# Moving one pair's ordering and DMA transposes from the first part to the end of step 10

## The chip, the cores and the metric

The kernel runs on one core of one Trainium2 chip. The metric is the device time of one execution in microseconds (us). A profiled execution also has a span, which in these runs is 1.8 us shorter than the time (411.0 against 412.8 us in the profile of before). TensorE is called PE, VectorE DVE, ScalarE ACT, GpSimd POOL, SyncE SP. PSUM is the memory, in banks, that PE writes its results into.

## The reference

Attention for 8 batches of 12 heads (sequence 448, head size 64), with one extra `exp(-m)` in the softmax denominator, then two matrix layers with an exact GELU between them:

```python
scores = scale * np.matmul(q, k.transpose(0, 1, 3, 2))
m = np.max(scores, axis=-1, keepdims=True)
e = np.exp(scores - m)
attn = e / (np.sum(e, axis=-1, keepdims=True) + np.exp(-m) + 1e-09)
attn_out = np.matmul(attn, v)
x = attn_out.transpose(0, 2, 1, 3).reshape(B * S, H * D)     # 3584 x 768
h = x @ w_in                                                 # 768 x 2048
out = (0.5 * h * (1.0 + erf(h / sqrt(2)))) @ w_out           # 2048 x 768
```

## The kernel before

The work goes in steps, one per pair of heads (6 pairs per batch, 48 steps). A step's scores run on PE between pieces of the matrix layers of the batch before. From batch 2 on, q and k are transposed by DMA rather than by PE. For batch 2 they first have to be put in order by pairs on DVE, into borrowed memory: buffers `hbuf0` and `hbuf1`, which hold the first layer's output in other phases, and a small tile `order`.

```python
PARTS = (0, 3, 4, NPAIR)          # batch 2: pairs 0-2, pair 3, pairs 4-5

def fetch_part(b, i):
    c0, c1 = PARTS[i:i + 2]
    for w in range(2):            # q, then k
        order_by_pairs(b, w, c0, c1, (1, 0, None)[i])   # hbuf1, hbuf0, order
        transpose_on_dma(b, w, c0, c1)                  # issued by SyncE
...
# fetch_part(2, 0) before step 8; parts 1 and 2 inside steps 12 and 13
```

The second layer's tiles of batch 0 go through a pool of output buffers (`osb_pool`). The stores of the second layer's first three tiles of batch 0 (steps 8 to 10) are held, and go out on SyncE together with step 11's own:

```python
if b == 0 and nh == 0:
    held.append(store)
else:
    store()
    for f in held:
        f()
    held.clear()
```

So after step 11 all four buffers wait for eight stores, and step 12's copy into a fifth tile needs one of them back.

The softmax here doesn't subtract the row's maximum and nothing guards it: scores larger than these inputs give would overflow.

Of the kernel before, what the change touches and what calls it, by code (L numbers as in the profile page):

```python
# [10 lines left out]
FP16 = mybir.dt.float16  # L11
# [8 lines left out]
def kernel(  # L20
# [11 lines left out]
    B, H, S, D = q.shape  # L32
    DM = H * D
    DFF = moe_w_in.shape[1]
    P = 128
    NJ = 4
    PS = S // NJ
    NK = S // P
    NPAIR = H // 2
# [6 lines left out]
    NBURST = 8  # L46
# [19 lines left out]
    h_pool = ctx.enter_context(tc.tile_pool(name="h_pool", bufs=1))  # L66
# [37 lines left out]
    def load_pairs(tiles, name, src, b):  # L104

        n, nj = (PS, NJ) if src is q else (P, NK)
        tiles[b] = raw_pool.tile([n, H, nj, D], FP16, name=name)
        if b == 3:
            nc.vector.memset(tiles[b][:, 0, 0, 0:1], 0.0)
        dst = tiles[b].rearrange("p h j d -> p (h j d)").rearrange(  # L110
            "p (c j e d) -> p c j e d", c=NPAIR, j=nj, e=2)
        view = src[b, :, 0:n * nj].rearrange("(c e) (p j) d -> j e p c d", e=2, j=nj)
        for j in range(nj):
            for e in range(2):
                nc.gpsimd.dma_start(out=dst[:, :, j, e, :], in_=view[j, e])  # L115
# [9 lines left out]
    def load_left(tiles, src, b):  # L125

        n = 2 if b else 1
        view = src[b, :, NFULL:S].rearrange("(c i e) s d -> i e s c d", i=n, e=2)
        for i in range(n):
            dst = tiles[b % 2].rearrange("p (c i) x -> p i c x", i=n)[:, i]  # L130
            for e in range(2):
                x = slice(e * D, (e + 1) * D) if src is k else slice(0, D)
                nc.gpsimd.dma_start(out=dst[left_rows(b, i, e), :, x], in_=view[i, e])  # L133
# [25 lines left out]
    def load_q(b, *heads):  # L159
        load_heads(q_raw, raw_pool, "rawq", q, b, *heads)  # L160

    def load_k(b, *heads):
        load_heads(k_raw, raw_pool, "rawk", k, b, *heads)

    def load_v(b, *heads):
        load_heads(v_t, v_pool, "vn", v, b, *heads)
# [96 lines left out]
    def transpose_on_pe(b, c, main=True, left=True):  # L263
        tp = ps_bank.tile([P, S + NFULL + P], FP16, name="bank")
        if main:
            for e in range(2):
                r = slice(e * D, (e + 1) * D)
                for j in range(NJ):
                    nc.tensor.transpose(
                        tp[r, j * PS:(j + 1) * PS], q_raw[b][:, 2 * c + e, j, :], ident[0:PS, 0:PS])  # L270
            for e in range(2):
                r = slice(e * D, (e + 1) * D)
                for j in range(NK):
                    nc.tensor.transpose(
                        tp[r, S + j * P:S + (j + 1) * P], k_raw[b][:, 2 * c + e, j, :], ident)
        if left:
            for e in range(2):
                r = slice(e * D, (e + 1) * D)
                nc.tensor.transpose(tp[r, S + NFULL:], kl_raw[b % 2][:, c, r], ident)
        x = slice(0 if main else S + NFULL, S + NFULL + P if left else S + NFULL)  # L280
        nc.vector.tensor_copy(
            out=qt_t[b].rearrange("p (c x) -> p c x", c=NPAIR)[:, c, x], in_=tp[:, x])

    ordered = [{}, {}]

    def order_by_pairs(b, w, c0, c1, buf):

        nj, raw = ((NJ, q_raw), (NK, k_raw))[w]
        if w == 0:
            n = 2 * (c1 - c0)  # L290
            if buf is not None:
                spare = h_pool.tile([P, NBURST * S], FP16, name=f"hbuf{buf}")
            else:
                spare = order_pool.tile([P, n * (NJ + NK) * D], FP16, name="order")
            for i, (rows, chunks, x) in enumerate(((PS, NJ, 0), (P, NK, n * NJ * D))):
                ordered[i][b] = spare[0:rows, x:x + n * chunks * D].rearrange(
                    "p (h j d) -> p h j d", h=n, j=chunks)
        src = raw[b].rearrange("p (c e) j d -> p c e j d", e=2)
        dst = ordered[w][b].rearrange("p h j d -> p (h j d)").rearrange(
            "p (c j e d) -> p c j e d", j=nj, e=2, d=D)  # L300
        for e in range(2):
            nc.vector.tensor_copy(out=dst[:, :, :, e, :], in_=src[:, c0:c1, e])

    def transpose_on_dma(b, w, c0=0, c1=NPAIR):
        if b not in qt_t:
            alloc_qt(b)
        nj, raw = ((NJ, q_raw), (NK, k_raw))[w]
        raw = ordered[w].get(b, raw[b])
        nc.sync.dma_start_transpose(
            out=dma_views(b)[w][:, c0:c1].rearrange("p c (j s) -> p (c j) s", j=nj),  # L310
            in_=raw.rearrange("p h j d -> p (h j d)"),
        )
        if w == 1 and c0 == 0:
            nc.sync.dma_start_transpose(
                out=dma_views(b)[2], in_=kl_raw[b % 2].rearrange("p c x -> p (c x)"))
# [333 lines left out]
    def mlp1(b, f0, f1):  # L649
        return [lambda mid=None, fc=fc: layer1(b, fc, mid=mid) for fc in range(f0, f1)]  # L650

    def take(n):
        got = l2[:n]
        del l2[:n]
        return got

    def gelu_window(b, n):

        load_table(SET_GELU)
        ready = take(len(l2))  # L660
        for f in ready:
            f()
        if not ready:
            for i in range(FCH - n):
                if i < n:
                    gelu_burst(b, i, i + 1)
                layer1(b, n + i, direct=True)
        else:
            for f0 in range(0, n, n // 2):
                gelu_burst(b, f0, f0 + n // 2)  # L670
            for fc in range(n, FCH):
                layer1(b, fc, direct=True)
        load_table(SET_LN_EXP)
        l2.extend(layer2_items(b))
# [5 lines left out]
        start_step(s)  # L680
    PARTS = (0, 3, 4, NPAIR)

    def load_part(i):
        load_q(2, 2 * PARTS[i], 2 * PARTS[i + 1])
        load_k(2, 2 * PARTS[i], 2 * PARTS[i + 1])
# [17 lines left out]
    stage_left(v, 1, gate=True)  # L703
    stage_left(k, 2, gate=True)
    load_part(0)
    for i in range(2):
        load_w_out(0, i, 2)
# [3 lines left out]
    cast_left(v, 1)  # L711
    cast_left(k, 2)
    load_part(1)
    load_v(1, 8, H)
    load_part(2)
    first, second = mlp1(0, 0, 2)
    first()
# [4 lines left out]
    add_up(4)  # L722

    def fetch_part(b, i):
        c0, c1 = PARTS[i:i + 2]
        for w in range(2):
            order_by_pairs(b, w, c0, c1, (1, 0, None)[i])
            transpose_on_dma(b, w, c0, c1)

    def fetch(b, r):  # L730

        if r == (0 if b else 2) and b + 2 < B:
            load_v(b + 2)
            load_left(vl, v, b + 2)
        if b == 0 and r == -1:
            fetch_part(2, 0)
        elif b and r in (0, 1) and b + 2 < B:
            transpose_on_dma(b + 2, r)
        if r == 3 and b + 3 < B:
            load_pairs(q_raw, "rawq", q, b + 3)  # L740
            load_pairs(k_raw, "rawk", k, b + 3)
            load_left(kl_raw, k, b + 3)

    step(NPAIR + 1, mlp1(0, 2, 6))
    gelu_window(0, 6)
    fetch(0, -1)
    for s in range(NPAIR + 2, NSTEP + 1):
        b, r = divmod(s - 2 - NPAIR, NPAIR)

        half = NBURST // 2  # L750
        if b and r < 2:
            step(s, mlp1(b, half * r, half * (r + 1)))
        else:
            left = len(l2) - (0 if b == 0 else 1 if b % 2 == 0 else 2)
            n = left if r == NPAIR - 1 else max(1, left // (NPAIR - r))
            if b and r == 2:
                n = 2
            step(s, take(n), late=(s == NSTEP or r == (2 if b else 0)),
                 then=(lambda: fetch_part(2, r - 3)) if b == 0 and r in (4, 5) else None)
        if b == 0 and r == 0:  # L760
            transpose_on_pe(1, NPAIR - 1)
        fetch(b, r)
        if b and r == 1:
            gelu_window(b, 2 * half)
# [41 lines left out]
```

## Time and profile before

| | before |
|---|---|
| time, median of the 3 runs given first (lowest to highest) | 411.38 us (410.46 to 411.83) |
| the profiled run: time, span | 412.8 us, 411.0 us |
| PE busy | 396.9 us, 97% |
| PE idle between 54 and 90 us | 2.3 us, 1.79 of it in one hole at 71.5 to 73.3 us |

PE is back to back after 90 us, so the table is read from its idle time before that. The lines themselves stand in the prediction.

### The profile page before, as it was taken

To read this page: it belongs to the slowest core of one execution; us is meant where nothing else is said; L and a number is where in the kernel's file an instruction comes from. 1 tells how busy PE (TensorE), PEld (TensorE's weight loads), DVE (VectorE), ACT (ScalarE), POOL (GpSimd) and SP (SyncE) were. 2 spreads that over 40 slices of the span, in tenths; PEclk is the share of its full clock that TensorE was granted. 3 is DMA by queue.
4 is the path that set the end of the run, shared out by engine and by line. 5 is a ranking of instruction groups with operands and counts; after the bars stand their busy time and mean duration, and the time that the engine had idled before them with its cause. 6 is when DMAs were issued, how large, how long until landed. Compare 5 with 4: busy or idle time off the path is not lost.

```text
span 411.0 us, 11090 instructions
## 1 busy us (share of the span) xinstructions
PE 396.9 (97%) x4711; PEld 245.8 (60%) x4711; DVE 199.5 (49%) x486; ACT 297.8 (72%) x451; POOL 120.3 (29%) x168
## 2 busy tenths in 40 slices
PE   6889999899999999999999999999999999999996
PEld 2445865556656665666666666566566565565664
DVE  3887336683366614674256813576046732530021
ACT  5999889779797747978687756988588766634300
POOL 8752313477552381056400563030000000000000
PEclk9999999999999999999999999999999999999999
DMA  9999999999994995289921999149012010110022
GB/s 162 159 189 203 193 189 161 192 156 172 147 165 86 147 181 53 60 124 136 128 59 59 161 134 101 53 99 151 21 40 60 22 41 2 59 50 11 2 80 77
DMA packets 137634, 44.02 MB, mean 107 GB/s; under 512 B 118704, under 2 KB 137584, under 8 KB 137584
## 3 DMA queue, kind: packets, MB, share of 16 engines
q0 software_dynamic: 90352, 22.19, 60.6%
q1 hardware_dynamic: 46288, 20.44, 28.1%
q10 hardware_dynamic: 944, 0.67, 0.7%
q8 instruction: 37, 0.61, 0.6%
q14 instruction: 13, 0.11, 0.1%
HBM read 45.61 MB, written 11.01 MB: 138 GB/s over the span
## 4 chain that ended last, share of the span: by engine, by line
PE 79%; DMA 15%; POOL 3%; issue 1%; DVE 0%; ACT 0%; POOLq 0%; DVEq 0%
PE bank L261 63%; DMA w_out_sb<-in_moe_w_out_dram 7%; PE st L362 6%; PE bank L411 5%; DMA w_in_sb<-in_moe_w_in_dram 5%; DMA rawq<-in_q_dram 2%; PE st L433 2%; PE st L261 2%; DMA tqk<-hbuf 2%; PE bank L426 1%; POOL rawk L99 1%; PE st L411 1%; POOL rawq L99 1%; POOL w_in_sb L173 0%; POOL klraw L133 0%
## 5 line engine op out<-in xcount | busy, mean ns | idle before, releaser
L261 PE MATMUL bank<-xt,w_in_sb 128*64 128x448 f16 x1536 | 152.1, 353 | 0.5 <-DVE xt L449 0.5
L350 ACT ACTIVATE et<-st,expb 128x896 f16<-128x896 f32 x144 | 134.4, 1005 | 24.2 <-PE st L362 23.8
L261 PEld LDWEIGHTS <-w_in_sb 128*64 128x64 f16 x1536 | 93.7, 110 | 54.3 <-issue 3.7
L261 PE MATMUL bank<-w_out_sb,gt_odd 128*64 128x384 f16 (+1 forms) x1056 | 88.1, 321 | 0.0
L530 DVE COPY osb<-bank 128x384 f32<-128x384 f32 (+1 forms) x56 | 31.0, 554 | 102.4 <-PE bank L261 102.0
L261 PEld LDWEIGHTS <-gt_odd 128*64 128x64 f16 x1056 | 58.8, 110 | 26.8 <-issue 2.1
L261 PE MATMUL bank<-w_out_sb,gt_even 128*64 128x384 f16 x768 | 68.8, 327 | 1.8 <-DMA w_out_sb<-in_moe_w_out_dram 1.8
L449 DVE TENSOR_TENSOR xt<-bank,rec 128x448 f16<-128x448 f32 x43 | 26.9, 625 | 75.1 <-PE bank L426 64.5
L261 PEld LDWEIGHTS <-gt_even 128*64 128x64 f16 x768 | 43.1, 110 | 24.4 <-issue 5.3
L473 ACT ACTIVATE gt_odd<-bank 128x448 f16<-128x448 f32 (+1 forms) x74 | 29.2, 394 | 21.7 <-PE bank L261 20.8
L362 PE MATMUL st<-tqk 64*64 64x448 f16 x576 | 41.8, 363 | 1.3 <-ACT et L350 0.4
L440 ACT ACTIVATE rec<-st,oneb 128x448 f32<-128x448 f32 x43 | 27.4, 639 | 16.8 <-PE st L433 16.0
L478 DVE COPY hbuf<-bank 128x448 f32<-128x448 f32 x54 | 33.5, 621 | 10.3 <-PE bank L261 8.7
L396 DVE TENSOR_TENSOR ksum<-ksum,el 64x448 f16<-64x448 f16 x96 | 37.0, 385 | 2.1
L115 POOL DMA_DIRECT2D rawq<-in_q_dram x40 | 30.6, 773 | 24.6 <-DMA vn<-in_v_dram 24.2
L99 POOL DMA_DIRECT2D vn<-in_v_dram x11 | 10.4, 947 | 88.2 <-PE bank L411 77.8
L396 DVE TENSOR_TENSOR ksum<-t,et 128x448 f16<-128x448 f16 x96 | 33.5, 384 | 0.7 <-ACT et L350 0.4
L396 DVE TENSOR_TENSOR t<-et 128x448 f16<-128x448 f16 x96 | 32.9, 385 | 1.0 <-ACT et L350 0.6
L473 ACT ACTIVATE gt_even<-bank 128x384 f16<-128x384 f32 x34 | 16.7, 491 | 22.1 <-PE bank L261 22.1
L411 PE MATMUL bank<-et,vn 128*64 128x448 f16 x258 | 32.2, 356 | 0.0
L350 ACT ACTIVATE el<-st,expb 128x448 f16<-128x448 f32 x48 | 30.8, 641 | 0.1
L362 PEld LDWEIGHTS <-tqk 64*64 64x64 f16 x576 | 15.3, 106 | 21.7 <-issue 17.4
(66 smaller groups left out, 284.7 us busy)
## 6 DMA issues: line engine op xcount, KB each, us to landing
vn<-in_v_dram POOLq DMA_DIRECT2D x6, 576.0 KB, 9.7
rawq<-in_q_dram POOLq DMA_DIRECT2D x40, 84.0 KB, 8.1
rawk<-in_k_dram POOLq DMA_DIRECT2D x33, 96.0 KB, 6.8
w_in_sb<-in_moe_w_in_dram POOLq DMA_DIRECT2D x4, 768.0 KB, 15.9
out_dram<-osb SPq DMA_DIRECT2D x15, 168.0 KB, 2.2
out_dram<-osb SPq DMA_DIRECT2D x16, 144.0 KB, 2.1
out_dram<-osb SPq DMA_DIRECT2D x16, 120.0 KB, 2.0
w_out_sb<-in_moe_w_out_dram POOLq DMA_DIRECT2D x2, 768.0 KB, 28.0
```

What stands on the lines that cost most here:

```text
L99: nc.gpsimd.dma_start(out=tiles[b][:, h0:h1], in_=src[b, h0:h1, 0:n * nj].rearrange("h (p j) d -> p h j d", j=nj),)
L115: nc.gpsimd.dma_start(out=dst[:, :, j, e, :], in_=view[j, e])
L261: nc.tensor.matmul(out[x], lhs[:, x], rhs, start=start, stop=stop)
L350: nc.scalar.activation(out=out, in_=in_, func=AF.Exp, bias=expb, scale=scale)
L362: nc.tensor.matmul(st[cols, e, 0:S], kt[r, j, cols], qt[r], start=True, stop=True)
L396: nc.vector.tensor_tensor(out=dst, in0=a, in1=x, op=ALU.add)
L411: nc.tensor.matmul(po_t[g][e * D:(e + 1) * D, 0:S], v_t[b][:, 2 * c + e, j, :], et[:, 2 * j + e], start=(first and j == 0), stop=(not firs ...
L440: nc.scalar.activation(out=rec_t[g], in_=den_t.pop(g)[:, 0:S], func=AF.Ln, bias=oneb, scale=1.0)
L449: nc.vector.tensor_tensor(out=xt_t[b][:, c, :], in0=po_t.pop(g)[:, 0:S], in1=rec_t.pop(g), op=ALU.mult)
L473: nc.scalar.activation(out=dst[:, 0, :], in_=ph[:, c0:c1], func=AF.Gelu)
L478: nc.vector.tensor_copy(out=h_t[b, i][:, n, :], in_=ph[:, 0:S])
L530: nc.vector.tensor_copy(out=osb[:, x:x + w], in_=po[:, 0:w])
```

## The change

Its intent: fewer DMA transposes beside the loading of w_out, by taking batch 2's third pair (pair 2) out of the first part. It is put in order and transposed at the end of step 10, when w_out has nearly landed. It shares hbuf0 with pair 3.

```diff
-    def order_by_pairs(b, w, c0, c1, buf):
+    def order_by_pairs(b, w, c0, c1, buf, x0):
...
+            x0 *= 2 * (NJ + NK) * D          # place inside the borrowed buffer
...
+    ORDERS = ((0, 2, 1, 0), (2, 3, 0, 0), (3, 4, 0, 1), (4, NPAIR, None, 0))
...
     def fetch_part(b, i):
-        c0, c1 = PARTS[i:i + 2]
+        c0, c1, home, x = ORDERS[i]
...
         if b == 0 and r == -1:
             fetch_part(2, 0)
+        elif b == 0 and r == 2:              # end of step 10
+            fetch_part(2, 1)
...
-                 then=(lambda: fetch_part(2, r - 3)) if b == 0 and r in (4, 5) else None)
+                 then=(lambda: fetch_part(2, r - 2)) if b == 0 and r in (4, 5) else None)
```

More of the change, by code (lines that the diff above doesn't have):

```diff
@@ L284 @@
     ordered = [{}, {}]
-    def order_by_pairs(b, w, c0, c1, buf):
+    spares = {}
+    def order_by_pairs(b, w, c0, c1, buf, x0):
         nj, raw = ((NJ, q_raw), (NK, k_raw))[w]
@@ L290, in order_by_pairs @@
             n = 2 * (c1 - c0)
-            if buf is not None:
-                spare = h_pool.tile([P, NBURST * S], FP16, name=f"hbuf{buf}")
+            if x0:
+                spare = spares[buf]
+            elif buf is not None:
+                spare = spares[buf] = h_pool.tile([P, NBURST * S], FP16, name=f"hbuf{buf}")
             else:
                 spare = order_pool.tile([P, n * (NJ + NK) * D], FP16, name="order")
-            for i, (rows, chunks, x) in enumerate(((PS, NJ, 0), (P, NK, n * NJ * D))):
+            x0 *= 2 * (NJ + NK) * D
+            for i, (rows, chunks, x) in enumerate(((PS, NJ, x0), (P, NK, x0 + n * NJ * D))):
                 ordered[i][b] = spare[0:rows, x:x + n * chunks * D].rearrange(
@@ L724, in fetch_part @@
     def fetch_part(b, i):
-        c0, c1 = PARTS[i:i + 2]
+        c0, c1, home, x = ORDERS[i]
         for w in range(2):
-            order_by_pairs(b, w, c0, c1, (1, 0, None)[i])
+            order_by_pairs(b, w, c0, c1, home, x)
             transpose_on_dma(b, w, c0, c1)
```

## The prediction

> **What bounds the kernel now.** I read the engine totals first. TensorE (PE) is busy 97% of the 411.0 us span, so only its 14.1 idle us can be won by moving transfers. I then cut the span into stretches and asked for each engine's busy time in each.
>
> ```profile
> PE 396.9 (97%) x4711; PEld 245.8 (60%) x4711; DVE 199.5 (49%) x486; ACT 297.8 (72%) x451; POOL 120.3 (29%) x168
> 0.00:54.00 54.00, 46.14 (x546) 28.29 (x548) 34.27 (x88) 46.05 (x80) 29.19 (x45) 0.97 1.29 182
> 54.00:70.00 16.00, 15.55 (x205) 9.27 (x202) 8.13 (x21) 15.15 (x23) 3.23 (x4) 1.00 1.37 175
> 70.00:74.00 4.00, 2.21 (x30) 1.50 (x26) 1.21 (x4) 3.07 (x5) 1.07 (x2) 1.00 2.06 119
> 74.00:86.00 12.00, 12.00 (x152) 6.99 (x149) 9.39 (x30) 10.76 (x15) 5.37 (x9) 1.00 1.58 189
> ```
>
> Columns of the last four: stretch, length, busy PE, weight loads, DVE, ACT, POOL, granted clock, DMA share, GB/s. Of PE's idle time 7.9 us lie before 54 us, where the change touches nothing. The change acts from 50 to 90 us, and there PE has one hole: 70 to 74, with 4.00 - 2.21 = 1.79 us idle. The chain of waits, in order of time, says what ends it and what comes next.
>
> ```profile
> 46.44 26.83 DMA w_out_sb<-in_moe_w_out_dram
> 73.27 0.04 issue
> 73.31 0.84 PE bank L261 x8
> ...
> 81.05 6.22 DMA tqk<-hbuf
> 87.28 0.04 DVEq L478
> 87.31 0.04 issue
> 87.36 0.64 DVE hbuf L478
> 87.99 0.04 issue
> 88.03 1.11 PE bank L261 x9
> ```
>
> So there are two transfer deadlines. At 73.3 PE waits for the last piece of w_out (step 11's half of the second layer needs it). At 87.3 VectorE (DVE) may not overwrite hbuf0 before the transpose of pair 3 has read it; DVE waited 0.73 us there. The third matmul group of step 14 needs the PSUM bank which that copy empties. PE loses almost nothing today, but the place has no slack: the copy ends at 88.00, the group starts at 88.03. After 90 us PE is back to back, so what is won or lost before 90 stays in the total.
>
> Then the DMA queues, microsecond by microsecond (three answers: 53 to 54, 66 to 67, 75 to 76; packets, MB, share).
>
> ```profile
> q0 software_dynamic: 425, 0.20, 150.4%
> ...
> q0 software_dynamic: 215, 0.13, 88.5%
> q1 hardware_dynamic: 217, 0.06, 41.1%
> ...
> q0 software_dynamic: 490, 0.19, 159.6%
> ```
>
> q0 carries the loads, w_out among them; q1 carries SyncE's transposes and stores. When q1 has transposes they go packet for packet with q0 (215 against 217), and q0 falls from 425 to 490 packets a us to about 200 to 250. First q1 packets: in the 55 to 56 slice, though the transpose was issued at 51.34; they run to about 72.7, just before w_out lands.
>
> **What the Trainium skill says.** "DMA: Bandwidth & Descriptors", section "Queues, rings and completion order", says that each DMA engine takes the queues in turn, packet by packet. The trace agrees: 215 beside 217. Its section "Issuing engines are not separate DMA queues" says that all queues share the same 16 engines; the halved q0 agrees. Its section "Latency and other measured facts" gives the hardware queue about 0.6 us to the first byte; here a store issued at 74.78 moves its first packet after 78, some 4 us later, with q0 full. The same section gives a DMA transpose 261 GB/s; here it moves 0.05 to 0.06 MB per us, some 55 GB/s, beside q0. I use the trace's values.
>
> **The change part by part.** No work is added but two small transposes' issue and two more DVE copies: at 50 us the four ordering copies become shorter, and four new ones stand on DVE's list after step 10's sums.
>
> (a) Removed at 50 to 55 us: pair 2's share of the copies, one third of 2 x 550 + 2 x 444 ns = 0.66 us. PE does not wait for DVE there: worth 0.
>
> (b) Removed from q1 before 73 us: pair 2 is 448 x 128 x 2 bytes of q and 384 x 128 x 2 of k, 213 KB, or 832 packets of 256 B. q1's first part is now 1344 + 1152 + 768 = 3264 packets (q, k, and the leftover rows of k), and becomes 2432. Summing q1's packets by us, number 2432 passes at 68.0. From there q0 would run alone. It still moves about 1146 packets, 0.5 MB, from 68.0 to the landing at 73.3; at the 0.2 MB per us that it has alone, that is 2.6 us. w_out would land near 70.7 instead of 73.3. PE needs it at about 71.5 (eight matmuls of the half start at 70.70 and last 0.82 us). So the 1.79 us should all or nearly all go.
>
> (c) Added on DVE at about 70.5: pair 2's four copies, as long as pair 3's today (two of q 0.35 us together, two of k 0.41 us: 0.7 us with the overlap). They precede step 10's last sums, which PE needs only in step 12, 6 us later; DVE is idle from 71.2 to 74.2. Worth 0.
>
> (d) Added on SyncE: two transposes issued at 70.9 and 72.1 (1.2 to 1.3 us each, as pair 3's). With a 4 us lag their first packets move near 75, after w_out. At some 250 packets a us beside q0 they take 3.3 us, to 78.2, and land near 79. PE first needs pair 2 in step 14, at 83.6: no wait.
>
> (e) The same two transposes now stand in front of the eight held stores. These are issued on eight completion semaphores in turn, each wait being for the transfer eight places back. In the new order the seventh and eighth stores wait for pair 2's q and k to land. Today the eight go out from 74.78 to 78.5, and pair 3's transpose waits for the first of them to land, 4.9 us after issue, so goes at 79.76. In the new kernel PE is 1.8 us earlier, so the first store goes at 73.4; its data queue behind pair 2 until 78.2, it lands at 78.3 to 79.4; the eighth store goes at 78.4 to 79.3. Pair 3's q transpose goes then at 78.9 to 79.7 rather than 79.76, its k 1.3 us later, and lands 6.2 us after that, at 86.4 to 87.2 rather than 87.3.
>
> (f) Sum. The first deadline frees 1.8 us of PE; the second comes only 0.1 to 0.9 us earlier and has no slack. PE then idles in step 14 for what is left, about 1.3 us. The gain is the smaller of the two: about 0.5 us. From the 411.38 median that makes 410.8.
>
> **The rivals.** First: the gain is kept whole, 1.8 us, 409.6. For it: if loads finish 2 us sooner, the stretch 77 to 84 is less crowded, and stores and pair 3 can land faster than today's 4.9 and 6.2 us. Against: the 4 us lag of q1 shows at each start in the loaded stretch, and total DMA work is the same. Second: the wait at 87.3 gets longer, as pair 2's packets are put before the stores and pair 3: with another us of delay 412.3. For it: q1 stands idle from about 68 or 70 to 75, and what it misses it must do later. Against: the stores are issued 1.4 us earlier. Third: the w_out wait does not shrink, as q0's packets are small at its end and a near standstill (87 q0 packets from 73 to 74) is not explained by q1; then the time stays at 411.4. Against: the standstill begins as w_out lands, so it does not delay it. A fourth, DVE too late for PE's banks in step 11, would cost at most the 0.7 us of the new copies; DVE's idle time after 71.2 speaks against it.
>
> **Range and chances.** Nothing here can move the time by 2% (8.2 us): PE holds 396.9 us of it, and both waits are under 2 us. Both deadlines in full, with the runs' own spread (410.46 to 411.83), give 409.5 to 412.1. Within 2%: 0.99.
>
> **What would show it right or wrong.** PE's hole in 70 to 74 falls from 1.79 us to under 0.4, and w_out lands before 72. q1's first part ends near 68. SyncE shows transposes at 70 to 73.5. The DVE copy into hbuf0 waits longer for the transpose than 0.73 us, 1.5 to 2.5, and PE shows a hole of about 1.3 us between 84 and 88. If that copy starts before 86.0, the first rival holds; if the chain still has w_out landing after 73, step (b) is wrong; if the copy starts after 88, the second rival holds.

## The result, and the profile after

The changed kernel took 412.66 us in the median (412.42 to 413.58, 4 runs), against 411.4 us for before (4 runs). The ratio is 1.0038, 95% interval 1.0014 to 1.0061. A ratio here is the mean time of one kernel's runs over that of the other's of the same rounds, so it is not quite the ratio of the medians quoted. In this call the change cost about 0.4%, and the prediction's range (409.5 to 412.1) did not hold the result.

The profile seems to say the contrary: its span is 410.6 us, shorter than before's 411.0. First the page's engine line, then the stretches that the prediction used (stretch, length, busy PE, weight loads, DVE, ACT, POOL, granted clock, DMA share, GB/s), of the changed kernel:

```profile
PE 396.8 (97%) x4711; PEld 245.9 (60%) x4711; DVE 199.3 (49%) x490; ACT 297.6 (72%) x451; POOL 120.1 (29%) x168
0.00:54.00 54.00, 46.38 (x548) 28.59 (x549) 33.44 (x88) 46.14 (x80) 29.00 (x45) 0.97 1.32 187
54.00:70.00 16.00, 15.55 (x206) 9.32 (x204) 8.38 (x22) 15.26 (x21) 3.86 (x5) 1.00 1.41 176
70.00:74.00 4.00, 4.00 (x54) 2.36 (x52) 2.79 (x11) 3.96 (x7) 2.54 (x4) 1.00 1.60 193
74.00:86.00 12.00, 10.26 (x126) 5.86 (x124) 8.36 (x26) 10.36 (x14) 6.59 (x10) 1.00 1.94 159
```

The hole of 1.79 us at 70 to 74 is gone, and one of 1.74 us has come between 74 and 86. The changed kernel's chain of waits tells where it comes from (start, length, what; lines of code from 286 on are numbered 5 higher than in before):

```profile
73.11 0.64 DVE xt L454
73.75 0.39 SPq L499
74.14 0.06 issue
74.19 5.47 DMA out_dram<-osb
79.78 0.56 DVE osb L535
...
82.61 0.39 DVE ksum L401
83.03 0.57 DVE osb L535
83.65 0.38 PE bank L431 x2
```

Step 12's copy of its output tile (L535, at 79.78) waits for a store that was issued at 74.19, because that store still reads the output buffer which the copy takes over. What comes next on DVE starts only after that copy (step 13's at 83.03), and at 83.65 PE gets the PSUM bank that step 13's copy has emptied. DVE and PE lines of the changed kernel's timeline, with the idle time before the instruction and what ended it in brackets:

```profile
79.78 0.56 DVE L535 COPY osb<-bank 128x384 f32<-128x384 f32 x1 [2.35 <-DMA out_dram<-osb]
83.65 0.38 PE L431 MATMUL bank<-el,vl 64*64 64x448 f16 x2 [1.74 <-DVE osb L535]
```

The same copy in the timeline of before:

```profile
79.98 0.56 DVE L530 COPY osb<-bank 128x384 f32<-128x384 f32 x1 [0.32 <-PE st L362]
```

It started at nearly the same time there. The profile puts its short wait down to PE, but the second store (issued at 75.19, 4.7 us to landing) landed at 79.90: the output buffers had no slack in before either. In the changed kernel step 11's output copy was 2.2 us earlier, and the landing of the second store (79.66) only 0.2 us.

Why the store was not earlier shows in SyncE's issues, of before and then of the changed kernel:

```profile
74.78 3.74 SPq L494 DMA_DIRECT2D out_dram<-osb  x8
79.76 1.19 SPq L309 DMA_TRANSPOSE tqk<-hbuf  x1
```

```profile
70.58 2.93 SPq L314 DMA_TRANSPOSE tqk<-hbuf  x2
73.60 5.82 SPq L499 DMA_DIRECT2D out_dram<-osb  x8
79.55 1.18 SPq L314 DMA_TRANSPOSE tqk<-hbuf  x1
```

SyncE is busy issuing pair 2's two transposes until 73.51. In before the first store left 0.59 us after step 11's output copy began (74.19 to 74.78), here 1.62 us (71.98 to 73.60). It then took 5.9 us to land instead of 4.9, landing after pair 2's transposes (78.62 and 79.03), which stand before it in the queue q1; run b3 below tests this order. One store even waited 1.2 us for pair 2 to land.

The DMA queues confirm the aim of the change. Of the changed kernel, from 66 to 67 and from 70 to 71 us:

```profile
q0 software_dynamic: 260, 0.11, 86.2%
q1 hardware_dynamic: 257, 0.07, 49.4%
...
q0 software_dynamic: 483, 0.19, 154.7%
```

The last packet of q1's first part is at 68.7, and from there q0 runs alone until pair 2's first packets at 73.8. The last piece of w_out landed at 70.56.

### The profile page after: what moved, and what is told of

Same layout as the page of the kernel before. It is cut to its first block, busy times and chain, and to the rows that moved or that the text cites. A ratio compares the mean times of both kernels' runs of the same rounds, so it can differ in the third digit from the quotient of the medians. Undisturbed runs are those within 1.5% of the kernel's fastest.

```text
span 410.6 us, 11100 instructions
## 1 busy us (share of the span) xinstructions
PE 396.8 (97%) x4711; PEld 245.9 (60%) x4711; DVE 199.3 (49%) x490; ACT 297.6 (72%) x451; POOL 120.1 (29%) x168
## 4 chain that ended last, share of the span: by engine, by line
PE 87%; ACT 6%; DMA 3%; DVE 2%; POOL 1%; issue 1%; SPq 0%; DVEq 0%; POOLq 0%
PE bank L261 69%; PE st L367 7%; PE bank L416 6%; ACT et L355 3%; PE st L438 2%; PE st L261 2%; DMA out_dram<-osb 2%; DMA klraw<-in_k_dram 1%; PE bank L431 1%; PE st L416 1%; ACT rec L448 1%; ACT rec L445 1%; ACT el L355 1%; DVE ksum L401 1%; DVE osb L535 0%
## 5 line engine op out<-in xcount | busy, mean ns | idle before, releaser
L535 DVE COPY osb<-bank 128x384 f32<-128x384 f32 (+1 forms) x56 | 31.0, 553 | 102.7 <-PE bank L261 100.3
L261 PEld LDWEIGHTS <-gt_odd 128*64 128x64 f16 x1056 | 58.8, 110 | 26.8 <-issue 2.1
L261 PE MATMUL bank<-w_out_sb,gt_even 128*64 128x384 f16 x768 | 68.7, 327 | 0.0
L454 DVE TENSOR_TENSOR xt<-bank,rec 128x448 f16<-128x448 f32 x43 | 26.9, 625 | 74.9 <-PE bank L431 64.1
L115 POOL DMA_DIRECT2D rawq<-in_q_dram x40 | 30.6, 772 | 27.2 <-DMA vn<-in_v_dram 25.9
L448 ACT ACTIVATE rec<-rec 128x448 f32<-128x448 f32 x48 | 28.0, 586 | 0.2
```

The source lines that it names most:

```text
L115: nc.gpsimd.dma_start(out=dst[:, :, j, e, :], in_=view[j, e])
L261: nc.tensor.matmul(out[x], lhs[:, x], rhs, start=start, stop=stop)
L448: nc.scalar.activation(out=rec_t[g], in_=rec_t[g], func=AF.Exp, scale=-1.0)
L454: nc.vector.tensor_tensor(out=xt_t[b][:, c, :], in0=po_t.pop(g)[:, 0:S], in1=rec_t.pop(g), op=ALU.mult)
L535: nc.vector.tensor_copy(out=osb[:, x:x + w], in_=po[:, 0:w])
```

## The experiments

All kernels were timed in 5 rounds beside before. Calls ran on different chips: a and b on one, c and d on another, e on a third. Only a, c and e had a full set of fresh runs of before (11); b and d had one each, and their ratios use those of a and c besides.

**a1: before, unchanged, against itself.** No edit.

> The kernel before, unchanged, against itself. Both theories: ratio 1.000, interval within 0.3%. The profile of before had a 1.79 us hole for w_out; if the hole depends on how early the loads of the first 45 us happen to run, this profile shows another size of it (0 to 1.8 us). If the ratio is off by 0.3% or more, the 0.38% recorded for the change is within the comparison's own error.

Measured: 412.03 us (410.41 to 415.01), ratio 1.0006 (0.9968 to 1.0043). The w_out hole at 74 us was 3.16 us in this profile. So it does change from run to run.

**a2: the changed kernel again.** No edit.

> The changed kernel, unchanged, against before on the same chip. Theory A (the w_out wait of 1.8 us is traded for a wait of DVE for the first two stores, whose 4 buffers are all in use; PE loses 1.74 us in step 13): ratio 0.998 to 1.001, profile again with a hole of 1 to 2 us at 80 to 84 us. Rival (the change really costs 0.38%): ratio 1.003 to 1.005, and the profile is over 1 us longer than that of before in this same call.

Measured: 412.82 us (411.56 to 415.75), ratio 1.0027 (0.9989 to 1.0064). The DVE copy waited 1.88 us for the store, PE 1.26 us at 84.2; there was also a w_out wait of 1.2 us, in step 8. The interval alone decides nothing; the hole is there again.

**a3 and a4: five output buffers, in the changed kernel and in before.**

```diff
-    osb_pool = ctx.enter_context(tc.tile_pool(name="osb_pool", bufs=4))
+    osb_pool = ctx.enter_context(tc.tile_pool(name="osb_pool", bufs=5))
```

> The changed kernel with 5 output buffers instead of 4, so that step 12's copy waits for no store. Theory A: the 2.3 us wait of DVE at 79.8 and PE's 1.7 us hole go, until the next deadline (hbuf0 read by pair 3's transpose, or step 13's copy which now waits for the same two stores); 0.5 to 1.7 us faster than the changed kernel, ratio to before 0.995 to 0.999. Rival (PE is then held by the hbuf0 deadline anyway): within 0.3 us of the changed kernel, with the hole moved to 84 to 88.

> Before with 5 output buffers. In before step 12's copy started at 79.98 with 0.3 us of waiting, so theory A expects 0 to 0.3 us, ratio 0.999 to 1.000: the buffer costs nothing as long as the w_out wait comes first. Rival (the buffers held before back as well): over 1 us faster.

Measured: a3 413.05 us, ratio 1.0025 (0.9991 to 1.0059), no gain over a2. a4 411.71 us, ratio 0.9985 (0.9956 to 1.0014), which decides between neither expectation. In a3 the wait for the store is gone and the deadline that the prediction had named takes its place. PE and DVE in its timeline:

```profile
88.56 2.46 PE L261 MATMUL bank<-xt,w_in_sb 128*64 128x448 f16 x24 [1.66 <-DVE hbuf L483]
87.88 0.62 DVE L483 COPY hbuf<-bank 128x448 f32<-128x448 f32 x1 [2.33 <-DMA tqk<-hbuf]
```

The rival of that run held: the hole moved to hbuf0, with the same size.

**b1: the changed kernel without either wait** (five output buffers, pair 3 ordered in hbuf1, which is free until step 15).

```diff
-    ORDERS = ((0, 2, 1, 0), (2, 3, 0, 0), (3, 4, 0, 1), (4, NPAIR, None, 0))
+    ORDERS = ((0, 2, 1, 0), (2, 3, 0, 0), (3, 4, 1, 2), (4, NPAIR, None, 0))   # and bufs=5
```

> The changed kernel with both new waits taken away: 5 output buffers, and pair 3 put in order in hbuf1 (free until step 15) instead of hbuf0 (overwritten in step 14). Theory A (what the change costs is these two waits behind a late q1): no PE wait for a DVE copy from 74 to 90 us, 1.3 to 2 us faster than the changed kernel, ratio to before 0.994 to 0.998. Rival (a third deadline, pair 2 or pair 3 needed by the scores of steps 14 and 15, comes next): the hole moves again and the ratio stays 1.000 to 1.003.

Measured: 410.82 us (410.48 to 411.19), ratio 0.9966 (0.9939 to 0.9993). No hole is left from 70 to 90 us:

```profile
70.00:74.00 4.00, 4.00 (x56) 2.37 (x50) 3.04 (x14) 3.96 (x7) 0.24 (x2) 1.00 1.65 190
74.00:86.00 12.00, 12.00 (x148) 7.48 (x146) 10.18 (x31) 11.83 (x17) 10.35 (x13) 1.00 1.83 166
86.00:90.00 4.00, 4.00 (x49) 2.44 (x46) 3.69 (x10) 1.89 (x4) 3.32 (x5) 1.00 1.96 179
```

**b2 and b3: pair 2 at the end of step 9, and of step 11.**

```diff
-        elif b == 0 and r == 2:
+        elif b == 0 and r == 1:        # b2;  r == 3 in b3
```

> The changed kernel with pair 2 moved to the end of step 9 instead of step 10, some 4.5 us earlier: its transposes are issued near 66 us and follow the first part in q1 with almost no gap. Theory A: pair 2 lands before the stores start, so there is no wait of DVE for stores; but pair 2 again takes turns with w_out, so its landing is as in before, with a hole of 0 to 3 us at 70 to 74 that changes from run to run; ratio 0.998 to 1.001. Rival (what the change costs lies in splitting the part in two, wherever the second is put): ratio stays 1.002 to 1.004.

Measured: 411.75 us, ratio 0.9992 (0.9964 to 1.0020). Its first store left at 73.51 and took 5.0 us, as in before. So it is mainly where the second part lies that costs, and not the splitting in two; the interval just reaches the rival's 1.002. The expectation of no wait was too good: 0.57 us of DVE for the store and 0.62 us of PE for hbuf0 remained.

> The changed kernel with pair 2 moved to the end of step 11, so that the eight held stores stand in front of its transposes in q1. Theory A (it is pair 2's place in front of the stores that holds the output buffers): the wait of DVE for stores at 78 to 80 us goes or shrinks to under 0.5 us; instead pair 2 lands 6 us after its issue near 77, at 83, and PE waits up to 2 us for it at step 14's scores, and pair 3 lands later too. Ratio 1.000 to 1.006. Rival (the stores are late because of q0's loads, not of pair 2): the wait for stores stays over 1.5 us.

Measured: 416.56 us, ratio 1.0109 (1.0078 to 1.0139), over the expected range. With the stores in front the first one took 4.9 us, and DVE waited 0.28 us for the buffer, as theory A has it. But pair 2 then came too late for step 14's scores, and the mean granted clock was 0.88 from 80 to 86 us, where this wait ends at 84.91, and 0.83 from 86 to 92:

```profile
84.91 0.59 PE L367 MATMUL st<-tqk 64*64 64x448 f16 x4 [2.90 <-DMA tqk<-hbuf]
```

**b4: before with both relaxations** (pairs 0 to 2 and pair 3 all in hbuf1, `bufs=5`).

> Before with the same two relaxations and the third pair in the first part, where it was. Theory A: only the w_out wait is left, 0 to 3.6 us from run to run, ratio 0.996 to 1.000, and b1 is faster than this one by the mean of that wait, 0.5 to 1.5 us. Rival (the w_out wait is rare without the profile running): b4 and b1 the same within 0.1%.

Measured: 410.31 us (409.63 to 411.01), ratio 0.9954 (0.9928 to 0.9979), as fast as b1. w_out was issued early in this profile (42.04 us) and there was no hole.

**c1: before a third time.**

> The kernel before once more, in one call with three others, because the last call had only one fresh run of before beside it. No drift: median 411 to 412.5, ratio 0.998 to 1.002. If it drifted, the ratio is off by as much as the last call's gains (0.997 or less). The profile gives another sample of the w_out hole; by the three samples so far it is there when the last piece of w_out is issued after 45.5 us and absent when it is issued before 44.7.

Measured: 412.22 us (411.19 to 413.28), ratio 1.0015 (0.9990 to 1.0039). Last piece of w_out issued at 44.78 us, hole 0.26 us, and 0.24 us of PE lost to the output buffers.

**c2 and c3: pair 3 in hbuf1 with four output buffers,** in the changed kernel and in before.

> The changed kernel with pair 3 in hbuf1 and still 4 output buffers: only the second of the two new waits is taken away. Theory A (the output-buffer wait comes first and is enough to lose the time): PE hole of 1.2 to 1.8 us at 80 to 84 us stays, ratio to before 1.001 to 1.004, like the changed kernel. Rival (hbuf0 alone is the cost, the output buffers follow): the hole is gone and the ratio falls to 0.996 to 0.999.

> Before with pair 3 in hbuf1 and 4 output buffers. If hbuf0 was the only wait near the edge in before (DVE waited 0.73 us there), ratio 0.997 to 0.999. If the output buffers bind too (the copy at 79.98 in before began as the stores landed), no gain: 0.999 to 1.001.

Measured: c2 412.63 us, ratio 1.0010 (0.9984 to 1.0036); c3 411.75 us, ratio 1.0024 (0.9985 to 1.0063), with single runs up to 416.16. In c2 the output-buffer hole stayed, as expected:

```profile
84.20 0.38 PE L431 MATMUL bank<-el,vl 64*64 64x448 f16 x2 [1.22 <-DVE osb L535]
```

a3 and c2 together: taking away one wait alone leaves the other.

**c4: b4 again.**

> Before with both relaxations again, now in one call with before itself. Holding up: ratio to before 0.995 to 0.998 and spread under 2 us as last time. Drift of the last call: 0.999 to 1.001. Its profile shows whether the w_out hole is there when the last piece of w_out is issued late.

Measured: 413.13 us, ratio 1.0033 (0.9993 to 1.0073). The six runs fall in two groups, 410.3 to 411.6 and 414.7 to 415.1. The profiled run is of the longer group, and has the w_out hole (2.74 us, issue at 46.23 us):

```profile
70.00:74.00 4.00, 1.61 (x20) 0.99 (x17) 1.29 (x4) 3.15 (x5) 0.62 (x1) 1.00 1.67 110
74.00:80.00 6.00, 5.65 (x52) 2.97 (x53) 2.21 (x9) 2.80 (x3) 4.21 (x6) 0.72 1.60 200
80.00:86.00 6.00, 6.00 (x78) 3.57 (x72) 5.71 (x20) 5.37 (x9) 1.72 (x3) 1.00 1.71 185
```

The mean granted clock is 0.72 for the 6 us from 74, which I estimate at a loss of 0.28 x 6 = 1.7 us on top of the hole. In a1 it was 0.72 as well. So b4's first gain was made in runs without the hole, as far as its one profile shows.

**d1 to d4: w_out made early, or late, in both kernels.** Fewer bytes ahead of it (d1 from before, d2 from the changed kernel; the result is wrong), or more (d3, d4; result right):

```diff
-    load_v(1, 0, 8)
+    v_t[1] = v_pool.tile([P, H, NK, D], FP16, name="vn")      # d1, d2
+    nc.vector.memset(v_t[1][:, 0:8], 0.0)
...
     load_v(1, 0, 8)
+    load_heads({}, extra_pool, "extra", v, 1, 0, 4)           # d3, d4: nobody reads it
```

> Before, with 384 KB less ahead of w_out (batch 1's values for heads 0 to 7 are zeroed on DVE instead of loaded, so the result is wrong on purpose). Cause (1): no w_out hole in any run, so a narrow spread (under 1.5 us) and a median near 410.5 to 411. Cause (2) says nothing of this run.

> The changed kernel with the same 384 KB less (result wrong on purpose). Cause (1): no w_out hole, but still DVE waits 1 to 2.5 us for the stores or the transposes, PE 1 to 2 us; 1 to 2 us slower than d1, median 411.7 to 413. Rival: with q0 lighter the stores land sooner, the wait is under 0.5 us and d2 equals d1 within 0.5 us.

> Before with 192 KB more ahead of w_out (values loaded once more into a buffer that nobody reads; result right). Cause (1): the w_out hole is there in every run, 2 to 4.5 us[...]; median 413.5 to 416.

> The changed kernel with the same 192 KB more (result right). Cause (1): w_out lands 2 us or more sooner than in d3, so its hole is 0 to 2 us and the output-buffer wait shrinks as PE comes later; 1 to 3 us faster than d3. Cause (2): slower than d3 or equal to it.

| | median (lowest to highest), us | ratio | PE holes in the profile, us |
|---|---|---|---|
| d1 | 412.15 (411.13 to 412.86) | 1.0012 | no w_out hole, none over 0.5 |
| d2 | 412.48 (411.22 to 413.44) | 1.0028 | 1.41 for hbuf0 |
| d3 | 413.52 (411.17 to 416.88) | 1.0044 | 1.00 for w_out, 1.41 for hbuf0 |
| d4 | 412.71 (411.96 to 414.01) | 1.0032 | 1.33 for w_out, 0.29 and 0.22 for the two new waits |

Cause (1) is that the change gains at w_out and loses at the two deadlines behind q1, so that its balance hangs on how late w_out is issued; cause (2) is that it costs time whatever w_out does. The signs are as cause (1) has them: the change loses when w_out is early (means 412.10 and 412.52) and wins when it is late (413.42 and 412.94). The differences are smaller than expected, and within the scatter of six runs, so the times of this pair of pairs lean to (1) and do not prove it. Several expectations missed. d2 came within 0.5 us of d1, as d2's rival has it, and its profile shows no wait for the stores, though PE lost 1.41 us for hbuf0. d3's w_out hole was 1.00 us and not 2 to 4.5, and d4's was no smaller. d1 was slower than expected; in its profile step 8's scores began late, at 55.31 us, but whether that is the reason is not shown.

**e1 and e2: b1 and the changed kernel side by side.** No new edit.

> The changed kernel with 5 output buffers and pair 3 in hbuf1, again. If its lack of waits is the reason for its first result: no PE hole from 60 to 90 us in the profile, median 410.3 to 411.6, spread under 2 us, ratio to before 0.995 to 0.999 (no w_out hole, because pair 2 is late, and no deadline behind q1). If the first result was a lucky call, as with before's version of it: ratio 1.000 to 1.004, some runs over 413.

> The changed kernel beside it on the same chip. If the two waits are its loss: 1 to 2.5 us slower than e1, ratio to before 1.000 to 1.005, PE hole of 1.2 to 1.8 us between 80 and 90 us in the profile. If not: within 0.5 us of e1.

Measured: e1 410.75 us (410.66 to 411.50), ratio 0.9983 (0.9951 to 1.0015); e2 412.89 us (411.70 to 415.15), ratio 1.0045 (1.0005 to 1.0085). Every run of e1 was faster than every run of e2. e2's profile lost 0.55 us to w_out and 0.64 us to the output buffers, less than expected:

```profile
71.24 0.84 PE L261 MATMUL bank<-w_out_sb,gt_even 128*64 128x384 f16 x8 [0.55 <-DMA w_out_sb<-in_moe_w_out_dram]
82.70 0.38 PE L431 MATMUL bank<-el,vl 64*64 64x448 f16 x2 [0.64 <-DVE osb L535]
```

b1 and e1 together are 12 runs between 410.48 and 411.50 us. This is the version that did best: the change with both new waits taken away. It beats the changed kernel clearly; against before its two ratios are 0.9966 (11 of the 12 runs of before behind it are those of call a) and 0.9983, the second with an interval that includes 1.

## Why the prediction was wrong

**Step (b), w_out, was right in kind and too large in size.** The hole went, and w_out landed at 70.56 where 70.7 was worked out. (By the packet counts number 2432 passes at 68.4 and not 68.0, which changes little.) But most of this was luck. The after profile issued the last piece 1.8 us earlier than the before profile, as the timelines of POOL in before and then in the changed kernel show:

```profile
46.44 0.74 POOL L181 DMA_DIRECT2D w_out_sb<-in_moe_w_out_dram  x1 [2.03 <-DMA rawq<-in_q_dram]
```

```profile
44.67 0.74 POOL L181 DMA_DIRECT2D w_out_sb<-in_moe_w_out_dram  x1 [1.94 <-DMA rawq<-in_q_dram]
```

So of the 2.7 us by which it landed earlier (73.27 to 70.56) only 0.9 us lie in a faster transfer. From issue to landing of the last piece, in all profiles but b2's, whose pair 2 was issued in between:

| last piece issued at, us | transposes of three pairs | of two pairs |
|---|---|---|
| 41.7 to 43.0 | 24.8 (b4), 24.8 (d1) | 24.9 (b1), 24.3 (d2) |
| 44.3 to 44.9 | 26.2 (c3), 24.3 (a4), 26.2 (c1) | 25.9 (after), 25.6 (c2) |
| 45.3 to 46.5 | 28.1 (a1), 28.1 (c4), 26.8 (before) | 25.9 (e2), 25.5 (b3), 25.9 (e1), 25.9 (a3) |
| 47.3 to 47.9 | 25.0 (d3) | 24.7 (a2), 24.4 (d4) |

In the third row the two columns are 0.9 to 2.6 us apart. In the others they are 0.6 us apart or less, or overlap. So the 2.6 us that w_out was to gain is the upper end of what the traces show.

**Step (f) failed first in its base.** It took 1.79 us, a hole seen in one execution of 412.8 us, off a median of 411.38 us that was made by other executions. Profiles with the transposes in before's order have w_out holes of 1.79 (before), 3.16 (a1), 0.26 (c1), 0 (a4), 0 (c3), 0 (b4) and 2.74 us (c4). Four of these seven have 0.3 us or less to win. The profiled runs can be taken apart: the time until step 8's scores, the holes from 60 to 90 us, and the stretch from step 8's scores to the first normalization of batch 2 (DVE, L449 or L454, near 106 us), in which the change's gains and waits lie.

| profile | span | step 8's scores at | holes | stretch to 106 us |
|---|---|---|---|---|
| before | 411.0 | 54.54 | 1.79 | 51.87 |
| a1 (before) | 413.2 | 53.48 | 3.16 (and 0.49 for w_out at 56.2) | 54.88 |
| c1 (before) | 409.4 | 53.81 | 0.50 | 50.93 |
| after | 410.6 | 54.30 | 1.74 | 51.66 |
| a2 (after) | 410.8 | 54.27 | 1.26 (and 1.19 for w_out at 57.6) | 52.25 |
| e2 (after) | 409.8 | 53.71 | 1.19 | 51.54 |
| a3, c2 (after, one wait less) | 411.4, 411.1 | 55.54, 55.38 | 1.66, 1.22 | 51.40, 51.14 |
| b1, e1 (after, both waits less) | 408.8, 409.7 | 55.05, 55.71 | 0, 0 | 49.54, 49.54 |

From that normalization to the last copy of an output tile it is 300.69 or 300.70 us in every profile, so the executions differ only before step 8's scores, in the stretch, and by 0.7 us at most in the last 4 us. The stretch is not blurred by the start, and so shows the effect better than the times do. The changed kernel is 2.0 to 2.7 us above the version without the two waits. With one wait taken away it is still 1.6 to 1.9 us above it. Before is 1.4 to 5.3 us above it, by the run (in a1 with the lower clock). In all rows above the last but a1's this is 0.2 to 0.9 us more than the holes; where the rest goes stays open. The new wait is there in all three profiles of the changed kernel (1.74, 1.26 and 0.64 us), and in two of them PE waited for w_out besides: the change did not make an end of that. In d1 to d4 the stretch is 50.10, 51.14, 52.47 and 52.14 us: 1.0 us lost with w_out early, 0.3 won with it late, as cause (1) has it, from one execution each.

Before without its hole would be 411.0 - 1.79 + 1.8 = 411.0 us; with the changed kernel's 1.74 us added it is 412.7, and 412.66 was measured. This sum closes, but it rests on single profiles, and the start alone moves by 2 us from run to run.

**Step (e) had the times nearly right and missed who waits for them.** It gave the first store's issue as 73.4 and its landing as 78.3 to 79.4 (measured 73.60 and 79.48), the transpose of pair 3 as 78.9 to 79.7 (measured 79.55), and even the store that waits for pair 2 was there. But it looked only for hbuf0's reader. The copy of step 12's output needs the buffer that the first stores read, all four being in use, and comes before the hbuf0 copy in DVE's order. In before this deadline stood at 79.90, with the copy starting at 79.98; the bracket named PE, and I had not asked when the stores landed. From the start of step 11's output copy to the first store's landing it was 5.5 us in before and 7.5 us after. So PE lost 1.74 us at 83.65, where step (f) had it lose about 1.3 us to hbuf0 between 84 and 88. The missed reader alone does not explain the loss: without it (a3) hbuf0 held PE for 1.66 us and the time was the same. Set against executions of before that have little or no hole to fill, either wait is a loss and not a remainder.

**The hbuf0 wait of 1.5 to 2.5 us did not show** in the changed kernel: its copy started at 86.52 without waiting for the transpose, as PE and DVE had already been held by the output buffer. It is real all the same: with five output buffers it is 2.33 us (a3). That there were two deadlines behind q1 and a limit to the gain was right; the one named was the second in line.

**Steps (a), (c) and (d) held.** DVE's four copies at 70.20 to 70.87 delayed nothing, and no step waited for pair 2 in the changed kernel. Of the prediction's signs those on the hole at 70 to 74, on w_out, on q1 and on SyncE came true, and those on hbuf0's copy and on a hole between 84 and 88 did not.

**The second rival** (412.3 us, "pair 2's packets are put before the stores") came nearest to the time, through the output buffers rather than hbuf0.

What stays open: how often before's timed runs have the hole, since only profiled executions show it; why w_out's last piece is issued anywhere from 42.0 to 47.4 us in the traces without the edits of d; and whether b1 would still beat a before that never has the hole, since b4 without it was as fast as b1. On the first the times give a hint: 7 of the 51 runs of before are over 414 us, and a1's profiled run with the largest hole is one of them; of the changed kernel's 16 runs 3 are, of the 12 of b1 and e1 none.

## What to carry to other kernels

When a wait is removed by moving transfers later, follow the queue in which they land, and list every reader of what stands behind them: a buffer pool with all its buffers in flight is a deadline even where the profile shows no wait on it. Before taking a hole off the time, check that it is in the runs that make the median, with more than one profile or with the profiled run's own time. Where two deadlines hang on the same late queue, relax both: either one alone bought nothing clear here (1.0025 and 1.0010), the two together about 2 us.

## What the Trainium skill lacked or had wrong

- "DMA: Bandwidth & Descriptors", section "Latency and other measured facts", gives about 0.6 us to the first byte on the hardware queue. Beside a full software queue the first packets came 3 us or more after the issue (pair 2's transpose issued at 70.58, first q1 packet at 73.8). Its 261 GB/s for a DMA transpose stood against 0.04 to 0.07 MB per us here in most slices, the queues going packet for packet. The page does not say what either becomes beside a loaded queue.
- "TensorE: Matmul & The Clock Gate", section "Part 1: The HAM clock gate", says that the clock falls to half after an idle window of about 3.4 us. In these runs holes of 1.79 us and less left the mean clock at 1.00 over the next 6 us, and holes of 2.74 us (c4) and 3.16 us (a1) were followed by 0.72 over 6 us, so the shortest hole that costs clock here lies below the page's window.
- No page says how far a loaded kernel's start varies: step 8's scores began anywhere from 53.5 to 55.7 us in executions of nearly the same program.
